# Sliding-window attention on one core: four heads per pipeline stage instead of two, and some small VectorE work placed elsewhere

## The chip, the cores and the metric

One core of a Trainium2 chip runs one program. The metric is the device time of one execution in microseconds, the median of several runs.

## What is computed

Three layers in a row, on 2 sequences of 768 tokens, 8 heads of 64, all in float32. The inputs are drawn at random; the window is 128 tokens and the first 4 tokens are sinks that every query sees.

```python
scores = scale * np.matmul(q, k.transpose(0, 1, 3, 2))
keep = is_sink | in_window
scores = np.where(keep, scores, -1000000000.0)
a = np.exp(scores - np.max(scores, axis=-1, keepdims=True))
a = a / (np.sum(a, axis=-1, keepdims=True) + 1e-09)
x = np.matmul(a, v)                      # 1536 tokens x 512
logits = x @ w_gate                      # 8 experts
# each token goes to the expert of its best pair that still has room (192 each),
# pairs taken by falling logit over all tokens
out[mask] = np.maximum(x[mask] @ w1[e], 0.0) @ w2[e]
x = out
return (x @ w_a) * (x @ w_b) @ w_out     # 512 -> 1536 -> 512
```

## The kernel before

The program has three parts, one behind the other. The attention (`Attention.run`, line 261) leaves the rows of `x` in a DRAM buffer `xd` and the gate's logits in a tile `L`. The routing (`Clear`) finds, in a fixed number of passes over `L`, which token goes where. The experts (`Experts.run`) gather the rows and do all the large products. Every order is written out by hand: each engine works through its instructions in the order in which the code issues them, and waits where an operand or a buffer isn't there yet.

The attention goes over 12 blocks of 128 queries, 6 for each sequence. A block sees its own 128 keys, the 128 before and, from the third block on, 32 keys of the start that hold the sinks: 288 columns. The first block of a sequence sees 128 columns and the second 256, without a sink slice. Queries and keys are each split into a rounded part and the remainder, so a score product is two matmuls into one PSUM tile (lines 281 and 282). `split` (line 248) does that for a block: VectorE casts, GpSimd subtracts (lines 256 to 259). For the first two blocks `split_half` (line 234) does it for four heads at a time: ScalarE casts for block 0 and VectorE for block 1, and GpSimd takes three of the four subtractions of line 245.

A stage `s` of the loop is two heads, so a block is four stages, and a group of four heads is two. In a stage the loop issues, in this order:
- every fourth stage, the loads of a later block on the SP queue (`load_v`, `load`), and the `split` of a later block;
- in odd stages `out_rows` of the group before the last: VectorE multiplies the finished rows by the reciprocal of the softmax sum (line 351), sums the logits (line 354), and the SP queue stores the rows into `xd` (line 355). For the first group of a block VectorE first adds 1e-9 to the sums (line 348) and takes the reciprocal (line 349);
- `scores` three stages ahead: for each of the two heads the two matmuls into a tile `sp` (three PSUM buffers, one for each head), VectorE's masked minimum `mn` (line 283), ScalarE's exponential with its sum (line 285);
- `turn` one stage ahead: four transposes of the probabilities on TensorE (line 297), one ScalarE copy (line 299);
- in odd stages `turn_sink`: the sink columns of four heads turned by matmuls 32 wide (line 307), a VectorE copy (line 309);
- `values` of two stages ago: products of 64 columns for each head (line 324), and with sinks one product 128 wide for the pair (line 327). In odd stages the finished tile `ot` goes to SBUF, on ScalarE for the first group of a block and on VectorE for the second (line 331);
- in even stages `rows`: two products that turn the group's output back to rows and add the gate logits (line 340), into the tile `x` (one buffer).

What else runs in certain stages hangs in a table handed to `run` (line 98): constants of the routing on GpSimd (stage 12), `rest`, four small VectorE operations (stage 30, lines 432 to 435), `lead(0)` to `lead(3)` (stages 36 to 42), and the first sums of the routing (44, 45). `lead` (line 760) loads two pieces of an expert's weights on the SP queue, casts one on ScalarE (line 752) and subtracts on GpSimd (line 758).

Of the kernel before, what the change touches and what calls it, by code (L numbers as in the profile page):

```python
# [22 lines left out]
E, FF = 8, 1024  # L23
# [38 lines left out]
def moe_attention_kernel(ctx: ExitStack, tc: tile.TileContext, kq, vN, vS, nums, wg, w12, wm, out,  # L62
# [22 lines left out]
    with ExitStack() as st:  # L85
        at.open(st, pre)
        at.load(0)

        warm = const.tile([128, 1], F32, name="warm")
        nc.vector.memset(warm, 0.0)  # L90
        nc.scalar.activation(warm, warm, AF.Exp)
        nc.scalar.dma_start(num, dram_ap(nums.bitcast(U32), 0, [[0, 128], [1, 4]]))
        make_identity(nc, ident)
        nc.vector.tensor_copy(numf[:, 0:4:2], num[:, 0:4:2])
        nc.vector.tensor_copy(numf[:, 1:4:2], num[:, 1:4:2].bitcast(I32))
        nc.vector.scalar_tensor_tensor(nv, numf[:, 1:4:2], 4294967296.0, numf[:, 0:4:2], op0=OP.mult, op1=OP.add)
        at.masks(nv[:, 0:1], nv[:, 1:2], slow)
        at.run({12: lambda: cl.constants(at.at), 30: lambda: cl.rest(), 36: lambda: ew.lead(0), 38: lambda: ew.lead(1), 40: lambda: ew.lead(2), 42: lambda: ew.lead(3), 44: lambda: cl.start(at), 45: lambda: cl.rest0(at.pp.tile([128, 128], F32, name="ts", bufs=1)[:, :E])})
# [43 lines left out]
class Attention:  # L142
# [118 lines left out]
    def run(self, extra):  # L261
        nc, at, pp, ident = self.nc, self.at, self.pp, self.ident
        blocks, V, VS, Q, KH, KL = self.blocks, self.V, self.VS, self.Q, self.KH, self.KL
        P, PK, MN, SM, T, TP, ST, OT, OS, XR, LP, RS, X = ({} for _ in range(13))

        nb = len(blocks)
        n = 4 * nb

        def scores(s):
            i, hp = divmod(s, 4)  # L270
            b, j = blocks[i]
            c0, w, co, cp, cs = kwin(j)
            if hp == 0:
                MN[i] = at.tile([128, H], F32, name="mn", bufs=3)
                SM[i] = at.tile([128, H], F32, name="sm", bufs=4)
            if hp % 2 == 0:
                P[s // 2] = at.tile([128, 4, 288], F32, name="p", bufs=3)
            p = P[s // 2]
            for h in (2 * hp, 2 * hp + 1):
# [5 lines left out]
                nc.scalar.activation(p[:, h % 4, :w], p[:, h % 4, :w], AF.Exp, bias=MN[i][:, h:h + 1], scale=-1.0,  # L285
                                     accum_out=SM[i][:, h:h + 1])

        def turn(s):
            i, hp = divmod(s, 4)
            c0, w, co, cp, cs = kwin(blocks[i][1])  # L290
            p = P[s // 2]
            tp = pp.tile([128, 4, 128], F32, name="tp", bufs=2)
            nsl = 2 if cp is None else 4
            for t in range(nsl):
                hl = 2 * (hp % 2) + t % 2
                c = co if t < 2 else cp
                nc.tensor.transpose(tp[:, t], p[:, hl, c:c + 128], ident)
            T[s] = at.tile([128, 4, 128], F32, name="t", bufs=5)
            nc.scalar.activation(T[s][:, :nsl], tp[:, :nsl], AF.Copy)
            if hp % 2 == 1 and cs is not None:  # L300
                PK[s // 2] = p[:, :, cs:cs + NS]

        def turn_sink(g):
            if g in PK:
                sp = pp.tile([128, 128], F32, name="ts", bufs=1)
                for h in range(4):
                    nc.tensor.matmul(sp[NS * h:NS * h + NS], PK[g][:, h], ident, start=True, stop=True, skip_group_check=True)
                ST[g] = at.tile([128, 128], F32, name="st", bufs=3)
                nc.vector.tensor_copy(ST[g], sp)

        def values(s):
            i, hp = divmod(s, 4)
            b, j = blocks[i]
            c0, w, co, cp, cs = kwin(j)
            if hp % 2 == 0:
                OT[s // 2] = (pp.tile([128, 288], F32, name="sp", bufs=3)[:, :256].rearrange("p (a n) -> p a n", a=2) if s == n - 2
                              else pp.tile([128, 2, 128], F32, name="ot", bufs=1))
            o = OT[s // 2]
            first = hp % 2 == 0
            mm = [(V[i], 0)] + ([(V[i - 1], 2)] if cp is not None else [])  # L320
            for k, (v, t) in enumerate(mm):
                for a in range(2):
                    h = 2 * hp + a
                    nc.tensor.matmul(o[64 * a:64 * a + 64, hp % 2], v[:, h * D:(h + 1) * D], T[s][:, t + a],
                                     start=first and k == 0, stop=cs is None and k == len(mm) - 1, skip_group_check=True)
            if cs is not None:
                nc.tensor.matmul(o[:, hp % 2], VS[b][:, hp // 2, hp % 2], ST[s // 2],
                                 start=False, stop=True, skip_group_check=True)
            if hp % 2:
                os = OS[s // 2] = at.tile([128, 2, 128], F32, name="os", bufs=2)  # L330
                (nc.vector.tensor_copy if hp == 3 else nc.scalar.copy)(os, OT.pop(s // 2))

        def rows(g):

            i, q = divmod(g, 2)
            x = X[g] = (pp.tile([128, 288], F32, name="sp", bufs=3).rearrange("p (a n) -> p a n", a=2) if g == n // 2 - 1
# [5 lines left out]
        def out_rows(g):  # L342
            i, q = divmod(g, 2)
            x = X.pop(g)
            if q == 0:
# [4 lines left out]
            hs = slice(4 * q, 4 * q + 4)  # L350
# [9 lines left out]
        for s in range(-3, n + 6):  # L360
            if (s + 3) % 4 == 0:
                i = (s + 3) // 4
# [4 lines left out]
            if (s + 3) % 4 == 1 and (s + 3) // 4 + 2 < nb and s > 0:  # L367
                self.split((s + 3) // 4 + 2, nc.gpsimd)
            if s - 5 >= 0 and s % 2 and (s - 5) // 2 != n // 2 - 2 and (s - 5) // 2 < n // 2:
                out_rows((s - 5) // 2)  # L370
            if s == n + 2:
                out_rows(n // 2 - 2)
            if s == -3:
                self.split_half(0, 0, nc.scalar.copy, nc.vector)()
                rest = self.split_half(0, 1, nc.scalar.copy, nc.gpsimd)
            if 0 <= s + 3 < n:
                scores(s + 3)
            if s == -3:
                rest()
            elif s == -2:  # L380
                self.split_half(1, 0, nc.vector.tensor_copy, nc.gpsimd)()
                self.second()
            elif s == -1:
                self.split_half(1, 1, nc.vector.tensor_copy, nc.gpsimd)()
            elif s == 0:
                self.split(2, nc.gpsimd)
                self.others()
            elif s == 40:
                self.wide()
            if 0 <= s + 1 < n:  # L390
                turn(s + 1)
            if s % 2 == 1 and 0 <= s < n:
                turn_sink(s // 2)
            if 0 <= s - 2 < n:
                values(s - 2)
            if s - 4 >= 0 and s % 2 == 0 and s != n and (s - 4) // 2 < n // 2:
                rows((s - 4) // 2)
            if s == n + 1:
                rows(n // 2 - 2)
            if s in extra:  # L400
                extra[s]()
# [690 lines left out]
```

## Time and profile before

| | us |
|---|---|
| median of 3 runs | 652.66 |
| lowest and highest | 652.20, 653.37 |
| the profiled execution | 653.24 |
| its span, first to last instruction | 651.5 |

| stretch of the profiled execution | from | to |
|---|---|---|
| start, until the scores of block 2 | 8.55 | 33.51 |
| attention, steady | 33.51 | 127.09 |
| tail, from the last group's scores to the last logits | 127.09 | 141.56 |
| routing | 141.56 | 179.49 |
| experts | 179.49 | 651.50 |

In the rows below PE is TensorE's matmuls and PEld its weight loads, DVE is VectorE, ACT is ScalarE, POOL is GpSimd, SP is the queue that issues loads and stores. Times are microseconds from the start of the span. TensorE's order is best read from the weight loads: each belongs to one matmul, and their starts aren't modelled.

### The profile page before, as it was taken

To read this page: it belongs to the slowest core of one execution; us is meant where nothing else is said; L and a number is where in the kernel's file an instruction comes from. 1 tells how busy PE (TensorE), PEld (TensorE's weight loads), DVE (VectorE), ACT (ScalarE), POOL (GpSimd) and SP (SyncE) were. 2 spreads that over 40 slices of the span, in tenths; PEclk is the share of its full clock that TensorE was granted. 3 is DMA by queue.
4 is the path that set the end of the run, shared out by engine and by line. 5 is a ranking of instruction groups with operands and counts; after the bars stand their busy time and mean duration, and the time that the engine had idled before them with its cause. 6 is when DMAs were issued, how large, how long until landed. Compare 5 with 4: busy or idle time off the path is not lost.

```text
span 651.5 us, 10366 instructions
## 1 busy us (share of the span) xinstructions
PE 589.8 (91%) x3804; PEld 544.4 (84%) x3804; DVE 373.0 (57%) x926; ACT 246.3 (38%) x639; POOL 105.2 (16%) x150
## 2 busy tenths in 40 slices
PE   2699969962299999999999999999999999999996
PEld 2478857851299999999999999999999999998885
DVE  6787795658534666756653355655665555722230
ACT  3566656820035445454432223223233223322330
POOL 3757663302311001000000000000000000003021
PEclk9999997985589999999999999999999999999998
DMA  9988673640076777777730023222232222102010
GB/s 187 226 162 198 139 168 99 193 122 9 24 207 212 239 253 235 259 227 246 235 101 2 33 64 98 65 73 89 66 98 64 65 69 93 33 1 97 1 65 33
DMA packets 50284, 79.04 MB, mean 121 GB/s; under 512 B 17456, under 2 KB 25648, under 8 KB 49712
## 3 DMA queue, kind: packets, MB, share of 16 engines
q1 hardware_dynamic: 48160, 71.99, 39.5%
q0 software_dynamic: 1920, 6.29, 3.1%
q8 instruction: 32, 0.52, 0.3%
q14 instruction: 28, 0.23, 0.1%
q10 hardware_dynamic: 144, 0.00, 0.0%
HBM read 71.98 MB, written 6.29 MB: 120 GB/s over the span
## 4 chain that ended last, share of the span: by engine, by line
PE 62%; issue 7%; POOL 1%; DVE 0%; ACT 0%; POOLq 0%
PE b L842 13%; PE b L897 10%; PE b L895 10%; PE b L896 10%; PE b L856 7%; PE b L857 3%; PE b L919 3%; PE b L918 3%; PE b L917 2%; POOL out L935 1%; PE b L832 1%; PE b L947 1%; DVE ys L866 0%; ACT y L868 0%; POOLq L1088 0%
## 5 line engine op out<-in xcount | busy, mean ns | idle before, releaser
L897 PE MATMUL b<-y,ml 128*128 128x384 f32 x384 | 128.6, 335 | 0.0
L895 PE MATMUL b<-y,mh 128*128 128x384 f32 x384 | 128.6, 335 | 0.0
L896 PE MATMUL b<-y,mh 128*128 128x384 f32 x384 | 128.5, 335 | 0.0
L842 PE MATMUL b<-xm,wr 128*128 128x192 f32 x512 | 89.1, 327 | 0.1
L842 PEld LDWEIGHTS b<-xm,wr 128*128 128x128 f32 x512 | 82.4, 190 | 0.3 <-issue 0.3
L856 PE MATMUL b<-hh,wh 128*128 128x384 f32 x256 | 79.5, 374 | 0.0
L895 PEld LDWEIGHTS b<-y,mh 128*128 128x128 f32 x384 | 72.1, 188 | 1.1
L896 PEld LDWEIGHTS b<-y,mh 128*128 128x128 f32 x384 | 72.1, 188 | 1.0
L897 PEld LDWEIGHTS b<-y,ml 128*128 128x128 f32 x384 | 72.1, 188 | 0.0
L758 DVE TENSOR_TENSOR wl<-wr,wh 128x512 fp32r<-128x512 f32 x60 | 41.5, 691 | 41.7 <-ACT wh L752 40.1
L935 POOL DMA_INDIRECT out<-xg,idx x6 | 6.2, 1041 | 361.9 <-ACT xg L933 361.0
L857 PE MATMUL b<-hh,wl 128*128 128x192 f32 x256 | 64.1, 250 | 0.0
L285 ACT ACTIVATE p<-p,mn 128x288 f32<-128x288 f32 (+2 forms) x96 | 47.9, 500 | 41.1 <-DVE mn L283 40.8
L281 PE MATMUL sp<-KH,q 128*128 128x288 f32 (+2 forms) x96 | 34.2, 369 | 22.7 <-DVE mn L283 13.1
L857 PEld LDWEIGHTS b<-hh,wl 128*128 128x128 f32 x256 | 48.9, 191 | 0.0
L856 PEld LDWEIGHTS b<-hh,wh 128*128 128x128 f32 x256 | 48.1, 188 | 0.0
L281 PEld LDWEIGHTS sp<-KH,q 128*128 128x128 f32 x96 | 20.4, 213 | 26.3 <-DVE mn L283 15.0
L283 DVE CUSTOM_DVE_ANT_0 p<-sp,mk 128x288 f32<-128x288 f32 (+2 forms) x96 | 36.8, 419 | 9.6 <-PE sp L282 9.3
L752 ACT ACTIVATE wh<-wr 128x512 fp32r<-128x512 f32 x64 | 39.9, 623 | 3.3 <-DMA wr<-in_w 3.3
L844 ACT ACTIVATE hh<-b 128x192 fp32r<-128x192 f32 x64 | 21.0, 328 | 46.8 <-PE b L842 46.8
L906 ACT ACTIVATE zz<-z 128x384 fp32r<-128x384 f32 x24 | 12.6, 525 | 58.8 <-DVE z L901 58.8
L257 POOL TENSOR_TENSOR KL<-kq,KH 128x1024 fp32r<-128x1024 f32 (+1 forms) x10 | 29.0, 2898 | 35.0 <-DVE KH L256 34.9
(246 smaller groups left out, 1067.8 us busy)
## 6 DMA issues: line engine op xcount, KB each, us to landing
wr<-in_w SPq DMA_DIRECT2D x128, 256.0 KB, 3.9
mr<-in_wm SPq DMA_DIRECT2D x36, 512.0 KB, 3.6
kq<-in_kq SPq DMA_DIRECT2D x12, 512.0 KB, 7.6
kq<-in_kq SPq DMA_DIRECT2D x8, 576.0 KB, 9.8
v<-in_vN SPq DMA_DIRECT2D x12, 256.0 KB, 4.9
xd<-xr SPq DMA_DIRECT2D x12, 256.0 KB, 3.2
kq<-in_kq SPq DMA_DIRECT2D x8, 256.0 KB, 6.2
xg<-xd,idx POOLq DMA_INDIRECT x12, 4.0
```

Of the source, the lines that this page charges most:

```text
L257: eng.tensor_tensor(kl, kr, kh.bitcast(F32), op=OP.subtract)
L281: nc.tensor.matmul(sp[:, :w], Q[i][:, h], KH[:, h, c0:c0 + w], start=True, stop=False)
L283: nc.vector.tensor_tensor_reduce(p[:, h % 4, :w], sp[:, :w], self.mask(j), -0.125, 1e30, op0=OP.add, op1=OP.min, accum_out=MN[i][:, h:h + 1])
L285: nc.scalar.activation(p[:, h % 4, :w], p[:, h % 4, :w], AF.Exp, bias=MN[i][:, h:h + 1], scale=-1.0, accum_out=SM[i][:, h:h + 1])
L752: self.nc.scalar.activation(self.W[u][0], self.R[u, 1], AF.Copy)
L758: (eng or self.nc.vector).tensor_tensor(lo, self.R.pop((u, 1)), hi.bitcast(F32), op=OP.subtract)
L842: nc.tensor.matmul(ps, w[:, 128 * k:128 * k + 128], x[:, k], start=k == 0, stop=k == 3)
L856: nc.tensor.matmul(ps, hi[:, 128 * d:128 * d + 128], hh, start=f == 0, stop=False, skip_group_check=True)
L857: nc.tensor.matmul(ps[:, 0], lo[:, 128 * d:128 * d + 128], hh[:, 0], start=False, stop=f == 7, skip_group_check=True)
L895: nc.tensor.matmul(p, hi[:, w, c], y[:, k, 0], start=k == 0, stop=False)
L896: nc.tensor.matmul(p, hi[:, w, c], y[:, k, 1], start=False, stop=False)
L897: nc.tensor.matmul(p, lo[:, w, c], y[:, k, 0], start=False, stop=k == 3)
```

## The change

Nothing of the arithmetic changes. A stage is now a group of four heads; iteration `it` issues `out_rows` of group `it - 3`, the scores of group `it + 1`, the turns of `it`, the values of `it - 1` and the rows of `it - 2`. ScalarE's instructions of a stage are held in lists and issued in a chosen order: two exponentials, the first copy of the turned probabilities, two exponentials, the second copy. The buffers keep their numbers. The add of 1e-9 goes from VectorE to ScalarE. In the first two blocks all subtractions are on VectorE and all casts on ScalarE. A `split` is issued behind the scores in even iterations. The table of other work goes to the iterations of the same groups: `rest` to 15, `lead` to 18 to 21.

```diff
-        at.run({12: lambda: cl.constants(at.at), 30: lambda: cl.rest(), 36: lambda: ew.lead(0), ...})
+        at.run({6: lambda: cl.constants(at.at), 15: lambda: cl.rest(), 18: lambda: ew.lead(0), 19: lambda: ew.lead(1), ...})
...
+        def scores(g):
+            i, q = divmod(g, 2)
...
+            out = []
+            for h in range(4 * q, 4 * q + 4):
                 sp = pp.tile([128, 288], F32, name="sp", bufs=3)
                 nc.tensor.matmul(sp[:, :w], Q[i][:, h], KH[:, h, c0:c0 + w], start=True, stop=False)
                 nc.tensor.matmul(sp[:, :w], Q[i][:, h], KL[:, h, c0:c0 + w], start=False, stop=True)
                 nc.vector.tensor_tensor_reduce(p[:, h % 4, :w], sp[:, :w], self.mask(j), -0.125, 1e30, op0=OP.add,
                                                op1=OP.min, accum_out=MN[i][:, h:h + 1])
+                out.append(lambda h=h: nc.scalar.activation(...))
+            return out
...
+            for e in range(2):
+                for k, (v, t) in enumerate(mm):
+                    for a in range(2):
+                        h = 4 * q + 2 * e + a
+                        nc.tensor.matmul(o[64 * a:64 * a + 64, e], v[:, h * D:(h + 1) * D], T[g, e][:, t + a], ...)
             if cs is not None:
+                for e in range(2):
+                    nc.tensor.matmul(o[:, e], VS[b][:, q, e], ST[g], start=False, stop=True, skip_group_check=True)
+            os = OS[g] = at.tile([128, 2, 128], F32, name="os", bufs=2)
+            return lambda: (nc.vector.tensor_copy if q else nc.scalar.copy)(os, o)
...
-                nc.vector.tensor_scalar(r[:, 0], SM[i], 1e-9, None, op0=OP.add)
+                nc.scalar.activation(r[:, 0], SM[i], AF.Identity, bias=tiny)
                 nc.vector.reciprocal(r[:, 1], r[:, 0])
...
+        self.split_half(0, 0, nc.scalar.copy, nc.vector)()
+        for it in range(-1, ng + 2):
+            if it % 2 and (it + 1) // 2 < nb:
+                i = (it + 1) // 2
                 if i + 1 < nb:
                     self.load_v(i + 1)
                 if i + 3 < nb:
                     self.load(i + 3)
+            if 0 <= it - 3:
+                out_rows(it - 3)
+            exps = scores(it + 1) if it + 1 < ng else []
+            for e in exps[:2]:
+                e()
+            if it == -1:
+                self.split_half(0, 1, nc.scalar.copy, nc.vector)()
+            elif it == 0:
                 self.second()
+                for half in range(2):
+                    self.split_half(1, half, nc.scalar.copy, nc.vector)()
+            elif it == 1:
+                self.others()
                 self.split(2, nc.gpsimd)
+            elif it % 2 == 0 and it // 2 + 2 < nb:
+                self.split(it // 2 + 2, nc.gpsimd)
+            ts = turn(it) if 0 <= it < ng else []
+            for e in ts[:1]:
+                e()
+            for e in exps[2:]:
+                e()
+            for e in ts[1:]:
+                e()
+            if 0 <= it < ng:
+                turn_sink(it)
+            if 0 <= it - 1 < ng:
+                copy = values(it - 1)
+            if 0 <= it - 2 < ng:
+                rows(it - 2)
+            if 0 <= it - 1 < ng:
+                copy()
+            if it == 20:
                 self.wide()
+            if it in extra:
+                extra[it]()
+        out_rows(ng - 1)
```

## Rows read from the trace of the kernel before

**Rows 1.** Table of stretches: length, busy time of each engine, granted clock, transfers.

```profile
core 0: us, PE busy (x) PEld busy (x) DVE busy (x) ACT busy (x) POOL busy (x), PEclk, DMA share, GB/s
8.55:33.51 24.96, 15.36 (x64) 12.12 (x64) 18.32 (x50) 12.15 (x47) 14.81 (x7) 1.00 1.08 226
33.51:70.47 36.96, 36.45 (x356) 29.77 (x356) 29.27 (x102) 26.49 (x84) 26.24 (x58) 1.00 0.78 168
70.47:107.92 37.45, 31.45 (x267) 24.78 (x266) 29.46 (x91) 20.16 (x70) 17.56 (x7) 0.91 0.61 133
107.92:127.09 19.17, 19.17 (x194) 15.67 (x193) 11.92 (x55) 15.01 (x46) 7.73 (x5) 1.00 0.65 192
127.09:141.56 14.47, 13.65 (x139) 10.34 (x137) 7.30 (x29) 6.62 (x20) 1.75 (x2) 1.00 0.36 94
...
179.49:651.50 472.01, 465.43 (x2664) 445.21 (x2664) 246.93 (x468) 161.35 (x364) 22.24 (x33) 0.99 0.37 115
```

**Rows 2.** Timeline of weight loads, one group: start, length, instruction, idle before and releaser.

```profile
48.82 0.19 PEld L281 LDWEIGHTS sp<-KH,q 128*128 128x128 f32 x1
...
49.33 0.48 PEld L297 LDWEIGHTS tp<-ident,p 128*128 128x128 f32 x4
49.98 0.42 PEld L324 LDWEIGHTS ot<-t,v 128*64 128x64 f32 x8 [0.17 <-ACT os L331]
50.56 0.30 PEld L327 LDWEIGHTS ot<-st,vs 128*128 128x128 f32 x2 [0.17 <-DVE rs L348]
50.78 0.55 PEld L340 LDWEIGHTS x<-ig,os 128*128 128x128 f32 x4
51.26 0.19 PEld L281 LDWEIGHTS sp<-KH,q 128*128 128x128 f32 x1
...
52.44 0.16 PEld L307 LDWEIGHTS ts<-ident,p 128*32 128x32 f32 x8 [0.17 <-issue]
52.80 0.42 PEld L324 LDWEIGHTS ot<-t,v 128*64 128x64 f32 x8 [0.20 <-issue]
...
53.60 0.19 PEld L281 LDWEIGHTS sp<-KH,q 128*128 128x128 f32 x1
```

**Rows 3.** Timeline of VectorE at three places, last a weight load that waits.

```profile
51.59 0.46 DVE L351 TENSOR_TENSOR xr<-x,rs 128x288 f32<-128x288 f32 x1 [0.84 <-PE x L340]
51.96 0.45 DVE L283 CUSTOM_DVE_ANT_0 p<-sp,mk 128x288 f32<-128x288 f32 x1
...
117.81 0.46 DVE L351 TENSOR_TENSOR xr<-x,rs 128x288 f32<-128x288 f32 x1 [1.30 <-PE x L340]
...
118.49 0.45 DVE L283 CUSTOM_DVE_ANT_0 p<-sp,mk 128x288 f32<-128x288 f32 x1
...
97.39 0.45 DVE L283 CUSTOM_DVE_ANT_0 p<-sp,mk 128x288 f32<-128x288 f32 x1
...
97.90 0.19 PEld L281 LDWEIGHTS sp<-KH,q 128*128 128x128 f32 x1 [4.00 <-DVE mn L283]
```

**Rows 4.** Groups by line and shape up to 33.51 us: busy, mean ns, idle before.

```profile
L259 POOL TENSOR_TENSOR q<-kq,q 64x1024 fp32r<-64x1024 f32 x2 | 4.8, 2406 | 0.2
L257 POOL TENSOR_TENSOR KL<-kq,KH 128x1280 fp32r<-128x1280 f32 x1 | 3.3, 3258 | 2.5 <-DVE KH L256 2.5
L191 DVE TENSOR_SCALAR mk<-mk 128x576 f32<-128x576 f32 x1 | 3.1, 3137 | 0.0
L245 DVE TENSOR_TENSOR KL<-kq,KH 128x512 fp32r<-128x512 f32 x1 | 0.7, 692 | 1.3 <-ACT KH L243 1.3
```

**Rows 5.** The add of line 348 (ns, min/median/max), and the first of `rest`.

```profile
L348 DVE TENSOR_SCALAR rs<-sm x12: 160/426/2043, 31.6 to 139.9; 128x8 f32<-128x8 f32 x12
...
92.18 2.26 DVE L432 SCALAR_TENSOR_TENSOR dg<-er,ak 128x128 f32<-128x128 f32 x1
```

**Rows 6.** Timeline of the weight loads of `lead` on SP and their casts on ScalarE.

```profile
114.13 0.63 ACT L752 ACTIVATE wh<-wr 128x512 fp32r<-128x512 f32 x1 [1.19 <-DMA wr<-in_w]
...
118.88 8.08 SPq L746 DMA_DIRECT2D wr<-in_w  x8
...
124.62 0.63 ACT L752 ACTIVATE wh<-wr 128x512 fp32r<-128x512 f32 x1 [2.08 <-DMA wr<-in_w]
```

More of the change, by code (lines that the diff above doesn't have):

```diff
@@ L97, in moe_attention_kernel @@
         at.masks(nv[:, 0:1], nv[:, 1:2], slow)
-        at.run({12: lambda: cl.constants(at.at), 30: lambda: cl.rest(), 36: lambda: ew.lead(0), 38: lambda: ew.lead(1), 40: lambda: ew.lead(2), 42: lambda: ew.lead(3), 44: lambda: cl.start(at), 45: lambda: cl.rest0(at.pp.tile([128, 128], F32, name="ts", bufs=1)[:, :E])})
+        at.run({6: lambda: cl.constants(at.at), 15: lambda: cl.rest(), 18: lambda: ew.lead(0), 19: lambda: ew.lead(1), 20: lambda: ew.lead(2), 21: lambda: ew.lead(3), 22: lambda: cl.start(at), 23: lambda: cl.rest0(at.pp.tile([128, 128], F32, name="ts", bufs=1)[:, :E])})
     redo = pre.tile([128, 1], I32, name="redo")
@@ L284, in scores @@
                                                op1=OP.min, accum_out=MN[i][:, h:h + 1])
[L285 to L289, printed above, removed]
+                out.append(lambda h=h: nc.scalar.activation(p[:, h % 4, :w], p[:, h % 4, :w], AF.Exp, bias=MN[i][:, h:h + 1],
+                                                            scale=-1.0, accum_out=SM[i][:, h:h + 1]))
@@ L290, in turn @@
+            return out
+        def turn(g):
+            i, q = divmod(g, 2)
             c0, w, co, cp, cs = kwin(blocks[i][1])
-            p = P[s // 2]
-            tp = pp.tile([128, 4, 128], F32, name="tp", bufs=2)
+            p = P[g]
             nsl = 2 if cp is None else 4
[L294 to L298, printed above, removed]
@@ L299, in turn @@
-            nc.scalar.activation(T[s][:, :nsl], tp[:, :nsl], AF.Copy)
-            if hp % 2 == 1 and cs is not None:
-                PK[s // 2] = p[:, :, cs:cs + NS]
+            out = []
+            for e in range(2):
+                tp = pp.tile([128, 4, 128], F32, name="tp", bufs=2)
+                for t in range(nsl):
+                    c = co if t < 2 else cp
+                    nc.tensor.transpose(tp[:, t], p[:, 2 * e + t % 2, c:c + 128], ident)
+                t = T[g, e] = at.tile([128, 4, 128], F32, name="t", bufs=5)
+                out.append(lambda t=t, tp=tp: nc.scalar.activation(t[:, :nsl], tp[:, :nsl], AF.Copy))
@@ L303, in turn_sink @@
+            return out
         def turn_sink(g):
-            if g in PK:
+            i, q = divmod(g, 2)
+            cs = kwin(blocks[i][1])[4]
+            if cs is not None:
                 sp = pp.tile([128, 128], F32, name="ts", bufs=1)
                 for h in range(4):
-                    nc.tensor.matmul(sp[NS * h:NS * h + NS], PK[g][:, h], ident, start=True, stop=True, skip_group_check=True)
+                    nc.tensor.matmul(sp[NS * h:NS * h + NS], P[g][:, h, cs:cs + NS], ident, start=True, stop=True, skip_group_check=True)
@@ L308, in turn_sink, with values @@
                 ST[g] = at.tile([128, 128], F32, name="st", bufs=3)
                 nc.vector.tensor_copy(ST[g], sp)
-        def values(s):
-            i, hp = divmod(s, 4)
+        def values(g):
+            i, q = divmod(g, 2)
             b, j = blocks[i]
             c0, w, co, cp, cs = kwin(j)
[L315 to L319, printed above, removed]
-            mm = [(V[i], 0)] + ([(V[i - 1], 2)] if cp is not None else [])
[L321 to L325, printed above, removed]
-            if cs is not None:
[L327 to L331, printed above, removed]
@@ L366, in run @@
                     self.load(i + 3)
[L367 to L381, printed above, removed]
+            if 0 <= it - 3:
[6 more added lines that the diff above has]
+            elif it == 0:
```

44 lines of the change are left out of this document (13 added, 31 removed).

## The prediction

> **What bounds the kernel now.** I read the table of stretches first [rows 1]. Behind 179.49 us TensorE is busy for 465.43 of 472.01 us at clock 0.99, and nothing that the change touches runs there. The routing between 141.56 and 179.49 us is not touched either. So only the attention, up to 141.56 us, can move the end, and what it loses or gains moves everything behind it by as much. In it the stretches differ: from 107.92 to 127.09 TensorE is busy without a break (19.17 of 19.17), from 33.51 to 70.47 nearly so (36.45 of 36.96), but the start uses 15.36 of 24.96 us and the stretch from 70.47 to 107.92 uses 31.45 of 37.45 at a mean clock of 0.91. So TensorE's own sequence is the bound in the steady part, and waits are in the start and in the middle.
>
> The second view is the weight loads of TensorE over one group of four heads [rows 2]: 48.82 to 53.60, 4.78 us. The brackets matter: TensorE stands 0.17 us at the first value product (128x64 tiles), 0.17 at the sink product (128x128), 0.17 at the sink turn (128x32) and 0.20 at the value product behind it, whichever releaser the row names; where the tile width stays (scores behind rows, turns behind scores) it stands not at all. The value products are issued twice in a group, so there are five such gaps (the fifth is like the second).
>
> The third view is VectorE beside it [rows 3]. A row product `x` is out 0.33 us after the next scores begin (51.26, 51.59), and the first score reduction follows 0.37 later (51.96). Where the logit sum stands between, it is 0.68 later (117.81, 118.49). From the start of a reduction until TensorE may write its score buffer again it takes 0.51 us (97.39, 97.90).
>
> **What the change does, part by part.**
>
> *Fewer switches.* With four heads per stage, the values of both pairs stand together. Of the five gaps in a group two go: turn to values, and values to sink or rows. 2 x 0.17 = 0.34, so TensorE's sequence for a group falls from 4.78 to 4.44 us. A group without sinks has four gaps and keeps two, the same 0.34.
>
> *A new wait.* `sp` still has three buffers, but a stage now has four heads. The fourth head's scores must wait until VectorE has reduced the first head's, and VectorE first does `out_rows` of three stages ago, whose `x` TensorE wrote just before. Two heads take 0.51 us (48.82 to 49.33) [rows 2], so TensorE is at the fourth head 0.77 us after the stage began. It may go on at 0.33 + 0.37 + 0.51 = 1.21 us in odd iterations and at 0.33 + 0.68 + 0.51 = 1.52 us in even ones [rows 2, 3]. That is 0.43 and 0.74 us of standing. Queued behind on TensorE are this stage's turns, the sink turn, the values and the rows: the whole sequence. An odd iteration becomes 4.87 us, an even one 5.18: in the mean 5.03 against 4.78. The switches saved are more than paid back. Bounds: nothing, if VectorE were there sooner, up to 1.0 if its products came late as well; I take the rows' own sum because the program's order leaves VectorE no choice.
>
> *Work out of GpSimd's way.* The add of 1e-9 takes 0.16 us undisturbed and up to 2.04 us [rows 5]; on ScalarE it should cost 0.2 us and hide there, but the reciprocal, and all that VectorE has queued behind it, now waits for ScalarE's queue. The four operations of `rest` stay on VectorE, at the end of iteration 15. In the kernel before, the first took 2.26 us beside a GpSimd subtraction [rows 5], and TensorE then stood 4.00 us, up to 97.90 [rows 3], with the lower clock after it. (The Trainium skill, "SBUF — State Buffer", section on the two separate sides, says that VectorE and GpSimd share one port pair, which the first comer holds for its whole instruction, against VectorE operations with two SBUF inputs or in a two-port mode. The rows agree, 2.26 us for 128 elements; by that rule `dg`, with two SBUF inputs, is held again wherever a split runs.) Block 9's subtractions begin about 3.2 us into iteration 14 and last about 5.1 (an estimate, a little under the 3.26 + 2.41 of a wider block) [rows 4], so until about 4.4 us into iteration 15, of 3.9 us and 4.1 us length. `rest` reaches VectorE at 2.3 us in iteration 15, waits to 4.4, and ends at 5.3, 1.2 into iteration 16. The fourth head's wait there becomes 1.6 us instead of 0.74. So most of the stall goes, not all.
>
> *ScalarE's wait for weights.* `lead(0)` and `lead(2)` copy a weight that is asked for only behind the `xd` store of the same iteration. The weight came 5.74 us after the issue (118.88 to 124.62) [rows 6]. Now the store's product is ready at about 0.8 us, the weight is asked for at 1.4 and lands at 7.2, which is 2.0 us into the next, odd iteration. There ScalarE still has to copy (0.55) and add (0.2), then VectorE takes the reciprocal (0.2) and the product (0.37): the first reduction starts at 3.3 instead of 0.70, 2.6 us late, all of it TensorE's. In the kernel before, ScalarE waited too (1.19 and 2.08 us) [rows 6] and TensorE did not, since no VectorE work of the row stage hung on ScalarE. For the first weight, whose wait was 0.9 us shorter, I take 1.7. Bounds: nothing, and 2.6 each.
>
> *The start.* It is a chain, from 8.55 us, which stays. Two exponentials and two casts on ScalarE to about 11.2, then two subtractions on VectorE at 0.69 [rows 4]: the second half of block 0 is ready at 12.6 (about 1 us later than now). Four score blocks and reductions to 15.0, masks 0.9, four subtractions at 0.69 and a little between them: block 1 is ready at 18.7. Two more exponentials, six mask copies on ScalarE to 21.3, the wide mask operation, which took 3.14 us beside GpSimd [rows 4], now about 0.4 before it, the cast of block 2 to 22.6, then GpSimd 3.26 + 2.41 [rows 4]: block 2 is ready at 28.4. TensorE's own work before it (stages 0 to 3) ends at the same time by its slower rows. So block 2's scores begin at 28.5 instead of 33.51: -5.0 us. Bounds: -6.5, if the copies overlap better; 0, if a load or the low speed of the first products holds block 2. GpSimd gets no subtraction of blocks 0 and 1; what hides VectorE's four is nothing, they are on the path and counted.
>
> **The sum**, by the stretches of rows 1, against the profiled 653.24 us (span 651.5):
> - start: -5.0.
> - 33.51 to 70.47, eight groups, 36.96 us: the first 3.65 and 0.9 for slower products (the start's take 15.36 us for 64 records, the next stretch's 36.45 for 356, though the clock column reads 1.00 in both), the second, with no sink product yet, 4.0 + 0.74, then three odd at 4.87 and three even at 5.18: 39.4. +2.5.
> - 70.47 to 107.92, seven groups, 37.45 us. With scores at 0.13 us each, turns at 0.12, values 0.42 for eight, sink product 0.22 for a pair, row product 0.48 [rows 2], and blocks 6 and 7 narrower and without sinks: TensorE's sequences 4.36, 3.53, 2.70, 3.17, 3.64, 4.01, 4.44 = 25.9, and waits at the fourth head 0.32, 0.62, 0.44, 0.74, 0.49, 1.63, 0.43 = 4.7: 30.5. -6.9, most of it the 4.00 us stall and the slow stretch after it.
> - 107.92 to 127.09, four groups, 19.17 us: 5.18 + 4.87 + 5.18 + 4.87 and 1.7 + 2.6 for the weights: 24.4. +5.2.
> - the tail, 14.47 us: 5.18 for the last scores, 3.4 for a stage without them, 1.6 for the last values, 2.4 from them to the last logits: 12.6. -1.9.
>
> Together -6.1: the profiled execution would take 647.1. The median of the runs shown, 652.66, is 0.6 below that execution, so I predict 646.5.
>
> **Rivals.**
> - *The fourth head does not wait.* Then all its waits go, 4.3 + 4.7 + 2.3 + 0.7 = 12 us: 634.5. For it: VectorE is busy for only 11.92 of 19.17 us where TensorE is the bound [rows 1]. Against it: the order on VectorE is fixed, and the product in front of the reduction needs a TensorE result that is 0.33 us old at best. Chance 0.08.
> - *The stalls bring the clock down (slower than before).* The middle stretch ran at 0.91, which is 0.09 x 37.45 = 3.4 us lost behind one stall of 4.00 us. Now TensorE stands for 1.6, 2.1 and 3.0 us in iterations 16, 19 and 21. If a stall of 1.6 is enough, three times 3.4 gives +10: 656.7; if only the two longer ones are, 653.3. Against it: the stalls are shorter than the one that did it, and no row here shows where it begins. Chance 0.11.
> - *The start does not pay.* Block 2 begins when it did, because the loads or TensorE's slow first products set it (the transfer engines are busy the whole time, share 1.08): 651.5. Chance 0.10.
> - *The add is moved but VectorE gains nothing by it.* If ScalarE reaches the add half a microsecond late in each of the twelve odd iterations, VectorE waits there and TensorE behind it: +6, 652.5. Against it: ScalarE is busy for 15.01 of 19.17 us even where it copies weights [rows 1]. Chance 0.06.
>
> **How the numbers follow.** The forecast, 646.5, has 0.65, with a range of its own of 641 to 651: the start by 2, the wait per group by 0.1 us over 23 groups, the weights by 3. For 8 in 10 I leave out the first rival (0.08), the upper half of the second and the forecast's own tails: 640 to 654. A measurement of this kernel tells about 0.2% from no change, 1.3 us. Faster than 651.4: 0.63 from the forecast, 0.08 from the first rival, 0.08 from the lower sides of the others: 0.79. Slower than 654.0: 0.08 from the second rival and 0.03 from the last two: 0.11. The rest, 0.10, lies between.
>
> **What would show it.** In the profile of the changed kernel: three gaps of 0.17 to 0.20 us at TensorE in a group instead of five; a wait of the fourth head's first score product for VectorE's `mn`, 0.4 to 0.8 us, in nearly every group, and group periods that alternate around 4.9 and 5.2 us; block 2's scores at about 28.5 us; a short VectorE hold at `dg`; a wait of the reciprocal for ScalarE behind the first and third weight; the last logits at about 135.4 us. If the periods are near 4.5, the first rival holds; if weight loads show the lower clock behind iteration 16, 19 or 21, the second; if block 2 begins near 33, the third. The prediction is wrong if the periods lie above 5.3 or if the clock falls.

## The result and the profile after

The change made the kernel slower: 656.52 us (median of 5 runs, 655.07 to 656.67) against 652.66 (5 runs, 651.37 to 653.73), a ratio of 1.0053 with a 95% interval of 1.0035 to 1.0072. Forecast was 646.5, with a range of 640 to 654. The profiled execution of the changed kernel has a span of 654.8 us, against 651.5 before.

The table of stretches of the changed kernel, cut where the same groups of four heads begin as in [rows 1], with the columns of that table.

```profile
8.62:34.52 25.90, 12.47 (x67) 10.49 (x68) 15.64 (x49) 14.16 (x52) 10.64 (x4) 0.87 1.08 224
34.52:74.85 40.33, 37.75 (x369) 32.02 (x369) 25.86 (x98) 27.57 (x88) 22.03 (x56) 0.96 0.70 150
74.85:105.74 30.89, 27.34 (x267) 22.98 (x265) 22.36 (x87) 21.70 (x77) 20.14 (x9) 1.00 0.75 161
105.74:131.74 26.00, 20.41 (x195) 16.98 (x194) 12.74 (x53) 15.67 (x48) 8.88 (x5) 0.93 0.54 163
131.74:144.44 12.70, 11.42 (x121) 9.48 (x119) 6.79 (x26) 5.77 (x17) 1.74 (x2) 1.00 0.27 64
```

Beside the forecast this gives, in us:

| stretch | before | forecast | after | after less forecast |
|---|---|---|---|---|
| start, to the scores of block 2 | 24.96 | 19.95 | 25.90 | +6.0 |
| blocks 2 to 5 | 36.96 | 39.4 | 40.33 | +0.9 |
| blocks 6 to 8 and half of 9 | 37.45 | 30.5 | 30.89 | +0.4 |
| the next four groups | 19.17 | 24.4 | 26.00 | +1.6 |
| tail | 14.47 | 12.6 | 12.70 | +0.1 |

Four of the five rows came out within 1.6 us of the forecast. The start did not: it was to give 5.0 us and took 0.9. The timeline of weight loads of the changed kernel shows where (start, length, instruction, idle before and releaser):

```profile
33.64 0.98 PEld L341 LDWEIGHTS x<-ig,os 128*128 128x128 f32 x4 [8.53 <-issue]
34.52 0.34 PEld L282 LDWEIGHTS sp<-KH,q 128*128 128x128 f32 x1
...
39.73 0.19 PEld L282 LDWEIGHTS sp<-KH,q 128*128 128x128 f32 x1
```

TensorE stands for 8.53 us ahead of its first row product (line 341), with the scores of block 2 queued behind it. The name in the bracket is `issue`, so the row alone doesn't tell what was late. The view of the product's weight tile `ig` does (who idled until what; the time from issue to landing of its loads):

```profile
  DMA ig<-in_wg: 8.3, 1
...
DMA to landing us min/median/max: 11.0/11.2/11.3
```

`ig` holds the gate's weights, which two loads of 8 KB each bring. The SP queue of the changed kernel in that time (start, time to issue, line, how many):

```profile
19.78 0.55 SPq L228 DMA_DIRECT2D v<-in_vN  x1
20.66 1.12 SPq L220 DMA_DIRECT2D kq<-in_kq  x2
21.83 1.29 SPq L193 DMA_DIRECT2D ig<-in_wg  x2
```

and of the kernel before:

```profile
19.70 1.66 SPq L193 DMA_DIRECT2D ig<-in_wg  x2
21.40 0.60 SPq L228 DMA_DIRECT2D v<-in_vN  x1
22.11 1.13 SPq L220 DMA_DIRECT2D kq<-in_kq  x2
```

The two gate loads are issued by `others` (line 193). Before, `others` ran ahead of the loads of values and keys; now it runs in iteration 1 behind them. The two loads left 2.1 us later, and they landed 11.2 us after the issue, behind block 4's keys, instead of 6.2. (The Trainium skill, "DMA: Bandwidth & Descriptors", section on queues, rings and completion order, says that each engine takes the descriptors of a ring in order; the two traces agree, 11.2 us behind the keys and 6.2 ahead of them.)

In the steady part the changed kernel does what the forecast said [rows 2, 3]. One group of four heads, weight loads:

```profile
54.58 0.19 PEld L282 LDWEIGHTS sp<-KH,q 128*128 128x128 f32 x1
...
55.91 0.19 PEld L282 LDWEIGHTS sp<-KH,q 128*128 128x128 f32 x1 [0.50 <-DVE mn L284]
...
57.25 0.16 PEld L311 LDWEIGHTS ts<-ident,p 128*32 128x32 f32 x8 [0.17 <-issue]
57.61 0.85 PEld L326 LDWEIGHTS ot<-t,v 128*64 128x64 f32 x16 [0.20 <-issue]
58.63 0.52 PEld L330 LDWEIGHTS ot<-st,vs 128*128 128x128 f32 x4 [0.17 <-issue]
...
59.55 0.19 PEld L282 LDWEIGHTS sp<-KH,q 128*128 128x128 f32 x1
...
61.06 0.19 PEld L282 LDWEIGHTS sp<-KH,q 128*128 128x128 f32 x1 [0.67 <-DVE mn L284]
```

Three gaps of 0.17 to 0.20 us are left of five, and the fourth head waits 0.50 or 0.67 us for VectorE's reduction (forecast 0.43 and 0.74). The periods are 4.97 and 5.15 (forecast 4.87 and 5.18), against 4.78 before.

### The profile page after: what moved, and what is told of

Read it like the earlier page. It is cut to its first block, busy times and chain, and to the rows that moved or that the text cites. A ratio compares the mean times of both kernels' runs of the same rounds, so it can differ in the third digit from the quotient of the medians.

```text
span 654.8 us, 10355 instructions
## 1 busy us (share of the span) xinstructions
PE 583.6 (89%) x3804; PEld 544.2 (83%) x3804; DVE 359.9 (55%) x913; ACT 250.9 (38%) x655; POOL 100.4 (15%) x148
## 4 chain that ended last, share of the span: by engine, by line
PE 62%; issue 7%; POOL 1%; DVE 0%; ACT 0%; POOLq 0%
PE b L845 13%; PE b L900 10%; PE b L898 10%; PE b L899 10%; PE b L859 7%; PE b L860 3%; PE b L922 3%; PE b L921 2%; PE b L920 2%; POOL out L938 1%; PE b L835 1%; PE b L950 1%; DVE ys L869 0%; ACT y L871 0%; POOLq L1091 0%
## 5 line engine op out<-in xcount | busy, mean ns | idle before, releaser
L909 ACT ACTIVATE zz<-z 128x384 fp32r<-128x384 f32 x24 | 12.6, 525 | 58.8 <-DVE z L904 58.8
```

## The experiments

All are edits of the changed kernel, except where an edit of the kernel before is named. "Group" is four heads; its time is read from the first score product of one to the first of the next.

### The start: where the gate loads stand on the SP queue

**e1_gate_load_first.** The two gate loads leave `others` for a function of their own, called in iteration 0, ahead of block 4's keys.

```diff
+        def gate():
...
             elif it == 0:
                 self.second()
+                self.gate()
...
```

> Only the place of the two small gate-weight loads on the SP queue is changed: issued in iteration 0, ahead of block 4's keys, as in the kernel before. Theory (the start lost its gain because the first row product waited for these loads behind 1.2 MB of keys): they land near 26 us, TensorE stands 1 to 2 us instead of 8.5, block 2's scores begin at 28 to 29 us instead of 34.5, and the clock does not fall there; 6 to 7 us less than the changed kernel's 656.5, so 649.5 to 650.5. Rival (the start is held by block 2's keys, GpSimd's subtractions or slow products anyway): block 2 begins at 32 or later and the time is 654 or more.

Measured: 652.12 us (650.22 to 653.35), a ratio to before of 0.9997 (0.9983 to 1.001). Block 2's scores begin at 28.27 us, but the row product ahead of them still stands for 1.99 us, and the products behind run at the slow pace: the group takes 7.22 us instead of 4.55. So the loads' place is the cause of the 8.53 us, but mending it gave 4.4 us by the medians, where 6 to 7 were expected.

**e9_gate_at_once.** The same loads ahead of the first value load, before the loop starts, so that no row product can wait for them.

```diff
         self.load(2)
+        self.gate()
         self.load_v(0)
```

> The changed kernel with the two gate loads issued on the SP queue ahead of the first value load, before the loop. In the earlier run with them in iteration 0 the row products still stood 1.99, 0.60 and 1.07 us in the start. Theory (the queue position of these two loads is the whole failed step of the start): no row product waits for the gate; block 2's scores at 28.2 us, the group behind them at 34.4 (39.73 in the changed kernel), so 5.3 us less: 650.5 to 651.5, since the two stalls of 2.98 and 2.19 us at the weights stay. Rival (the half-speed products of the start set it, whenever the gate comes): the group behind starts at 35.5 as in the earlier run and the time stays at 652.

Measured: 651.76 us (650.78 to 654.18), 0.999 (0.9978 to 1.0002), no better than the first try. (Its profiled execution took 654.18 us, 2.4 more than the median.) Its weight loads:

```profile
28.32 0.19 PEld L284 LDWEIGHTS sp<-KH,q 128*128 128x128 f32 x1 [2.41 <-POOL q L261]
...
31.12 0.29 PEld L284 LDWEIGHTS sp<-KH,q 128*128 128x128 f32 x1 [1.51 <-DVE mn L286]
...
33.60 1.58 PEld L328 LDWEIGHTS ot<-t,v 128*64 128x64 f32 x16 [0.33 <-issue]
...
35.95 0.19 PEld L284 LDWEIGHTS sp<-KH,q 128*128 128x128 f32 x1
```

VectorE's timeline beside it:

```profile
28.39 0.69 DVE L258 CAST KH<-kq 128x1024 fp32r<-128x1024 f32 x1 [3.94 <-DMA kq<-in_kq]
```

The gate loads land 11.3 us after the issue, behind six loads of keys, but well before they are needed. The row product's stall is gone, and block 2's scores begin at 28.32 us, released by GpSimd's last subtraction: the 28.5 of the forecast. But the next group begins at 35.95, not at 33.05 as the forecast's sum has it (28.5 and a first group of 3.65 + 0.9). Two things take the 7.63 us of that group. Sixteen weight loads of value products take 1.58 us instead of 0.85; the table of stretches of this run agrees (granted clock in the third column from the end):

```profile
26.00:28.30 2.30, 0.13 (x2) 0.00 (x0) 0.00 (x0) 0.75 (x3) 2.27 (x1) 1.00 1.24 255
28.30:31.00 2.70, 1.63 (x6) 1.28 (x6) 2.51 (x8) 0.00 (x0) 1.78 (x1) 0.55 0.97 197
```

0.55 is near the lower of the two levels, 1.2 of 2.4 GHz; ahead of it TensorE stood 2.41 us. And the fourth head waits 1.51 us, since VectorE stood 3.94 us for block 3's keys, whose loads the queue now issues at 20.03 us instead of 16.54. Of the two theories for this run the second held in its numbers: with the gate on time, the slow products set the time, and beside them VectorE's wait, which it had not named.

### The score buffer

**e2_rows_behind.** VectorE's work on the rows is issued behind this iteration's score reductions instead of ahead of them; the buffers stay three.

```diff
-            if 0 <= it - 3:
-                out_rows(it - 3)
             exps = scores(it + 1) if it + 1 < ng else []
             for e in exps[:2]:
                 e()
+            if 0 <= it - 3:
+                out_rows(it - 3)
```

> Only the row stage's VectorE and ScalarE work (add, reciprocal, product, logit sum) is issued behind the score reductions instead of ahead of them. Theory (the fourth head waits for VectorE because the row product stands in front of the first reduction): the wait falls from 0.50 and 0.67 us to about 0.3 in every group, and the two long stalls behind the expert weights (2.98 and 2.19 us) go, since the reciprocal no longer stands in front of the reductions: 8 to 9 us less, 647.5 to 648.5. Rival (the order on VectorE is not what sets the wait): 655 or more, waits of 0.5 us and over stay.

Measured: 648.6 us (648.47 to 649.35), 0.9942 (0.9921 to 0.9963), 8 us below the changed kernel. The wait is 0.26 or 0.27 us in most groups (in three it is 1.01, 1.43 and 0.65), as here:

```profile
58.10 0.19 PEld L282 LDWEIGHTS sp<-KH,q 128*128 128x128 f32 x1
...
59.20 0.19 PEld L282 LDWEIGHTS sp<-KH,q 128*128 128x128 f32 x1 [0.26 <-DVE mn L284]
...
62.84 0.19 PEld L282 LDWEIGHTS sp<-KH,q 128*128 128x128 f32 x1
```

The period is 4.74 in place of 4.97 and 5.15, and the two stalls at the expert weights are gone; in their place row products wait 1.22 and 1.54 us. So VectorE's order makes the larger part of the wait; the 0.26 us that stay are those of three buffers, and go with a fourth (the next run).

**e3_sp4.** A fourth score buffer; for its room in PSUM the tiles `ts` and `x` share a bank.

```diff
+        self.tx = self.pp.tile([128, 512], F32, name="tx")
...
-                sp = pp.tile([128, 288], F32, name="sp", bufs=3)
+                sp = pp.tile([128, 288], F32, name="sp", bufs=4)
...
-                sp = pp.tile([128, 128], F32, name="ts", bufs=1)
+                sp = self.tx[:, 288:416]
...
```

> A fourth score buffer: the sink turn and the row product share one PSUM bank, and the bank that comes free becomes a fourth buffer; the order stays. Theory (the three buffers are the cause of the wait at the fourth head): all waits of TensorE for a reduction go, also those of 2.98, 2.19, 1.22 and 1.02 us, the group period falls to about 4.45 us, 13 to 16 us less: 640.5 to 643.5, with the 8.5 us at the first row product still in it. Rival (VectorE's and ScalarE's own work per stage is the bound as soon as the wait goes): the period stays at 4.9 to 5.1, no more than 4 us less, 652 or more.

Measured: 647.88 us (647.09 to 649.65), 0.9937 (0.9915 to 0.996), 4 us above what was expected. The periods are the expected ones, 4.45 and 4.53, with no wait at the fourth head. But the shared bank makes new waits wherever VectorE is late:

```profile
98.00 0.54 PEld L342 LDWEIGHTS tx<-ig,os 128*128 128x128 f32 x4 [2.14 <-DVE st L314]
...
111.10 0.16 PEld L312 LDWEIGHTS tx<-ident,p 128*32 128x32 f32 x8 [1.67 <-DVE xr L353]
```

The first stands behind `rest`, whose first operation took 2.40 us there; the second behind the first expert weight. A fourth buffer takes away the wait that is there in every group and leaves those whose cause is elsewhere.

### The stalls at the expert weights

In the changed kernel, ScalarE at the two of them, iterations 19 and 21:

```profile
112.69 0.63 ACT L755 ACTIVATE wh<-wr 128x512 fp32r<-128x512 f32 x1 [2.31 <-DMA wr<-in_w]
...
124.53 0.63 ACT L755 ACTIVATE wh<-wr 128x512 fp32r<-128x512 f32 x1 [1.52 <-DMA wr<-in_w]
125.06 0.28 ACT L350 ACTIVATE rs<-sm,tiny 128x8 f32<-128x8 f32 x1
```

VectorE at the second:

```profile
125.38 0.20 DVE L351 RECIPROCAL rs<-rs 128x8 f32<-128x8 f32 x1 [0.79 <-ACT rs L350]
```

The weight loads that wait, at the first and at the second:

```profile
114.72 0.19 PEld L282 LDWEIGHTS sp<-KH,q 128*128 128x128 f32 x1 [2.98 <-DVE mn L284]
...
126.56 0.27 PEld L282 LDWEIGHTS sp<-KH,q 128*128 128x128 f32 x1 [2.19 <-DVE mn L284]
```

It is the chain that the prediction gave: the weight is late, ScalarE waits to copy it, the add stands behind the copy, the reciprocal behind the add, the reduction behind that, TensorE behind the reduction.

**e4_weights_sooner.** The loads of the first three weights two iterations sooner.

```diff
+16: lambda: [ew.load_w(u, a) for u in range(3) for a in range(2)],
...
-        for a in range(2):
-            self.load_w(u, a)
         self.hi_w(u)
         self.lo_w(u, self.nc.gpsimd)
+        if u == 0:
+            for a in range(2):
+                self.load_w(3, a)
```

> Only the loads of the first three expert weights are issued two iterations sooner. Theory (ScalarE, waiting for a weight, holds the add, the reciprocal behind it, and so TensorE): the stalls of 2.98 and 2.19 us become 0.5, and the slow stretch behind the second goes: 5 to 6 us less, 650.5 to 651.5. Rival (these stalls come from GpSimd's weight subtraction holding VectorE): the stalls stay, 655.5 or more.

Measured: 651.69 us (650.48 to 654.57), 0.9994 (0.9979 to 1.001). The stall of 2.98 us became 0.56, but the other only went from 2.19 to 2.06, though ScalarE now copied in time. VectorE there:

```profile
120.33 0.90 DVE L201 TENSOR_TENSOR c<-nv 128x1 f32<-128x1 f32 x1
...
121.58 0.19 DVE L351 RECIPROCAL rs<-rs 128x8 f32<-128x8 f32 x1
```

Ahead of the reciprocal stands `wide`, five operations on a single column (lines 199 to 203) that iteration 20 issues last. One of them, 0.15 us in the changed kernel, took 0.90 beside GpSimd's subtraction of the weight.

**e10_three_mended.** The gate loads at once, the weights sooner, and `wide` ahead of the copy of `os`, where VectorE waits for TensorE anyhow. The order of the rest is the changed kernel's.

```diff
...
+            if it == 20:
+                self.wide()
             if 0 <= it - 1 < ng:
                 copy()
-            if it == 20:
-                self.wide()
```

> The changed kernel with three things mended and its order of work otherwise kept: the gate loads ahead of the first value load, the first three expert weights loaded two iterations sooner, and the five small VectorE operations of `wide` issued in iteration 20 ahead of the copy of os instead of behind it. With the weights sooner alone, the second stall (iteration 21) stayed at 2.06 us of 2.19; there the reciprocal followed the end of `wide` at 121.58, one of whose operations took 0.90 us beside GpSimd. Theory (that stall had two causes, the weight and `wide`): now the second stall is 0.5 to 0.7 us, and the time is 651 - 4 - 1.5: 645.0 to 646.5, about what the prediction gave. Rival (the add on ScalarE alone holds the reciprocal): the second stall stays at about 2 us and the time is 647.

Measured: 645.46 us (644.58 to 646.7), 0.9887 (0.9869 to 0.9905). The second stall is 0.57 us, as the first:

```profile
108.22 0.19 PEld L284 LDWEIGHTS sp<-KH,q 128*128 128x128 f32 x1 [0.57 <-DVE mn L286]
...
118.43 0.19 PEld L284 LDWEIGHTS sp<-KH,q 128*128 128x128 f32 x1 [0.57 <-DVE mn L286]
```

So that stall had two causes, one behind the other; the second showed only when the first was gone. The four groups that took 26.00 us take 20.41 here.

### The add, and `rest`

**e7_add_on_vector.** The add of 1e-9 back on VectorE.

```diff
-                nc.scalar.activation(r[:, 0], SM[i], AF.Identity, bias=tiny)
+                nc.vector.tensor_scalar(r[:, 0], SM[i], 1e-9, None, op0=OP.add)
```

> The changed kernel with the add of 1e-9 back on VectorE, nothing else. Theory (VectorE would be held there until GpSimd's key subtraction ends, 1.0 to 1.6 us into an odd iteration): the add takes 0.8 to 1.4 us in most odd iterations, the fourth head's wait there grows by as much, about 9 times, against 5 to 6 us saved behind the two expert weights: 3 to 7 us more than the changed kernel's 656.5. Rival (VectorE isn't held): the add takes 0.16 us and the time falls by 5 to 6, to 650.5 to 651.5.

Measured: 665.46 us (663.96 to 668.35), 1.0192 (1.0164 to 1.022), 9 us above the changed kernel, where 3 to 7 were expected. The add in the view of the tile `rs` (min/median/max ns):

```profile
L350 DVE TENSOR_SCALAR rs<-sm x12: 159/737/2044, 29.9 to 154.5; 128x8 f32<-128x8 f32 x12
```

The timeline of VectorE at one of the long adds:

```profile
100.72 2.00 DVE L350 TENSOR_SCALAR rs<-sm 128x8 f32<-128x8 f32 x1
...
103.42 0.45 DVE L284 CUSTOM_DVE_ANT_0 p<-sp,mk 128x288 f32<-128x288 f32 x1
```

Where GpSimd runs, the add takes up to 2.04 us, and the reductions stand behind it. Here TensorE's fourth head waits 2.44 us, the granted clock of the group is 0.78, and the group takes 7.71 us; odd groups whose add is held for only 0.73 us take 5.75 instead of 4.97. In the changed kernel ScalarE's twelve adds lie between 0.285 and 0.303 us. (The Trainium skill, "SBUF — State Buffer", section on who interferes with whom, says that operations like this one and like a cast can enter a mode that needs the port pair shared with GpSimd, and that the one that comes second is then blocked until the other's instruction is done. The rows agree: GpSimd's subtraction runs from 100.00 to 102.70 us, and the add, 0.16 us undisturbed [rows 5], from 100.72 to 102.72.) So in the new order the move of the add is worth 9 us; no run makes it in the order before.

**e6_before_rest_33.** The kernel before, with `rest` three stages later and nothing else.

```diff
-12: lambda: cl.constants(at.at), 30: lambda: cl.rest(),
+12: lambda: cl.constants(at.at), 33: lambda: cl.rest(),
```

> The kernel before, with one thing changed: the four small VectorE operations for the routing's constants in stage 33 instead of 30, when GpSimd has no subtraction running. Theory (the middle stretch lost about 7 us to these operations being held beside GpSimd and to the slow clock after it; the grouping has no part in that gain): 6 to 7 us less than before's 652.2, 645.5 to 646.5. Rival (the grouping itself made that gain, or another operation stalls there next): 651 or more.

Measured: 646.25 us (645.79 to 646.9), 0.9905 (0.9882 to 0.9928). In its table of stretches, the one that answers to 70.47 to 107.92 [rows 1]:

```profile
70.49:100.91 30.42, 28.45 (x267) 22.74 (x266) 26.41 (x87) 19.74 (x69) 16.67 (x7) 1.00 0.74 163
```

30.42 us, where the changed kernel has 30.89 and the kernel before 37.45. Its first operation of `rest` took 0.28 us, beside no GpSimd subtraction. So moving `rest` alone gives as much in the middle as the whole change; four heads in a stage aren't needed for it.

### Versions that beat both

**e5_all** (four score buffers, early gate and weight loads, `rest` in iteration 17), **e8_orders** (three buffers, rows behind the reductions, the same early loads and `rest`) and **e11_wide_ahead** (the same as e8_orders, with `wide` ahead of the copy). Their edits are those shown above, and:

```diff
-15: lambda: cl.rest(),
+17: lambda: cl.rest(),
```

> The changed kernel with four score buffers, the gate loads ahead of the values of block 0, the expert weights' loads two iterations sooner, and the four operations of the routing's constants in iteration 17, whose group has a sink turn so that VectorE comes to them later. Theory (the losses are these separate waits and add up): against the kernel with four buffers alone (647.9) the start gives 3 to 6, the two expert-weight stalls 3, the stretch at iterations 15 to 17 about 3: 636 to 640. Rival (one wait covers the next): 644 or more.

> The changed kernel with its three score buffers, but the row stage's VectorE work behind the reductions, the gate loads ahead of the values of block 0, the expert weights' loads two iterations sooner, the routing's constants in iteration 17. Theory: a wait of 0.26 us in every group stays, the other stalls go: against 648.6 of the kernel with the row stage behind, the start gives 3 to 6 and the expert weights and the constants 3 more: 639.5 to 643. Rival (one wait covers the next): 646 or more.

> The version with rows behind the reductions, early gate and weight loads and `rest` in iteration 17 (640.75), with `wide` issued in iteration 20 ahead of the copy of os. Its last long stall is 1.40 us at 113.33, where VectorE was in `wide` from 111.26 to 112.83. Theory (that stall is `wide`): it becomes about 0.3 and the time is 639.0 to 640.0. Rival (the stall is something else): no difference, 640.7.

Measured: 639.54 us (638.99 to 640.54), a ratio to before of 0.98 (0.9778 to 0.9822); 640.75 (639.18 to 642.3), 0.9818 (0.9787 to 0.9848); 640.54 (638.81 to 641.21), 0.9808 (0.9791 to 0.9825). The three can't be told apart. The first two lie within what was expected of them: the separate losses add up. In e11_wide_ahead the stall of 1.40 us in iteration 21 is gone and its group takes 4.74 us instead of 5.88, but the start came out 0.7 us longer in its profiled execution, and the time didn't show the gain; so that theory is shown for the stall and not for the time.

## Why the prediction was wrong

The span came out 9.4 us above the forecast for the profiled execution (647.1, its span 645.4): 6.0 in the start, 0.9, 0.4, 1.6 and 0.1 in the other stretches, 0.4 behind the attention.

**The step that failed is the start.** The prediction followed the chain over ScalarE, VectorE and GpSimd, and that chain came true: the second half of block 0 is ready at 12.61 us (forecast 12.6), and with the gate mended block 2's scores begin at 28.32 (28.5). What it left out are the DMAs inside `others`: its sentence "block 2 is ready at 28.4" speaks of the scores' operands, and "TensorE's own work before it (stages 0 to 3) ends at the same time" took for granted that the row products had theirs. Counted to the start of the group behind, 39.73 us against a forecast of 33.05, the miss is 6.7: 39.73 to 35.95, 3.8 us, is the gate loads' place (e9_gate_at_once), and 35.95 to 33.05, 2.9, is what stays when they are on time. Two things make that rest. VectorE's wait for block 3's keys, 1.51 us, was not in the sum. And the products were sized too small: the group's 7.63 us less that wait are 6.12, where the sum had 3.65 and 0.9 for their slowness, so the 0.9 measured 2.5. e5_all, whose four buffers leave no wait at the fourth head, shows the products alone, 6.41 us for the same group:

```profile
28.21 0.29 PEld L285 LDWEIGHTS sp<-KH,q 128*128 128x128 f32 x1 [3.77 <-POOL q L262]
...
34.62 0.19 PEld L285 LDWEIGHTS sp<-KH,q 128*128 128x128 f32 x1
```

In the changed kernel that group took 5.21 us, most of the 0.9 in the table's second row. Nor did TensorE's earlier work end when block 2 was ready: in e9_gate_at_once TensorE had stood for 2.41 us by then. (These parts are of single executions: by the medians, 656.52 and 651.76, the loads' place is worth 4.8 us, not 3.8.)

The bound at the worse end, "0, if a load or the low speed of the first products holds block 2", was the right one. The third rival was built on it, and a load did hold block 2, though the rival named none; block 2 began at 34.52 us, where the rival had it as before, at 33.51.

**The switches and the new wait: right.** 2 x 0.17 us less, 0.50 and 0.67 of standing, periods of 4.97 and 5.15. The rival that the fourth head doesn't wait is out; e2_rows_behind and e3_sp4 show that it would have paid.

**`rest`: right in kind, and the whole of the middle.** The hold came: VectorE's first operation of `rest` and its fourth in the timeline of the changed kernel:

```profile
93.85 1.97 DVE L435 SCALAR_TENSOR_TENSOR dg<-er,ak 128x128 f32<-128x128 f32 x1
...
96.31 0.17 DVE L438 CAST eh<-ef 128x8 bf16<-128x8 f32 x1
```

and the fourth in the kernel before:

```profile
94.91 1.90 DVE L435 CAST eh<-ef 128x8 bf16<-128x8 f32 x1
```

TensorE's weight loads that wait in that iteration and the next:

```profile
92.86 0.19 PEld L282 LDWEIGHTS sp<-KH,q 128*128 128x128 f32 x1 [1.22 <-DVE mn L284]
...
97.57 0.19 PEld L282 LDWEIGHTS sp<-KH,q 128*128 128x128 f32 x1 [1.02 <-DVE mn L284]
```

1.02 us of waiting, forecast 1.6, against 4.00 before [rows 3]. Before, `rest` was held twice, 2.26 us at its first operation [rows 5] and 1.90 at its fourth, behind GpSimd's two subtractions; the prediction named the first alone. Now there is one hold. That the stretch came out within 0.4 us is partly luck: the group ahead waited 1.22 us where the sum had 0.49, since VectorE's reciprocal there stood 0.36 us for ScalarE and its cast 0.30 us for keys. What the prediction did not say is that this gain doesn't need the grouping; e6_before_rest_33 has it alone.

**The expert weights: the chain right, their sum by luck, plus a clock.** The two stalls were forecast at 2.1 and 3.0 us and measured at 2.98 and 2.19. Each is off by 0.8 or 0.9 us, and the errors cancel: the prediction took the first weight's wait as the shorter, and ScalarE waited 2.31 us for the first and 1.52 for the second. The 1.6 us above the forecast are the lower clock behind the second one, in the table of stretches of the changed kernel:

```profile
114.70:118.40 3.70, 3.68 (x43) 3.15 (x43) 1.39 (x7) 3.36 (x11) 0.86 (x1) 1.00 0.00 0
...
126.50:131.70 5.20, 5.14 (x41) 4.25 (x42) 1.52 (x8) 3.34 (x11) 0.00 (x0) 0.67 0.56 191
```

A third of 5.20 us is 1.7. So the rival of the clock came true in one place out of three, at half the 3.4 us it was priced at; that "the clock falls" was one of the prediction's own signs of being wrong. Why 2.98 us of standing cost nothing here and 2.19 did stays open. It is not the place in the program, for at the same one in e1_gate_load_first the loads behind the stall are slow:

```profile
110.20 0.29 PEld L284 LDWEIGHTS sp<-KH,q 128*128 128x128 f32 x1 [3.11 <-DVE mn L286]
```

In e9_gate_at_once they are too, behind 2.78 us; of the 3.8 us gained at its start, 2.5 are left at the last row products (140.40 us against 142.88). `wide`, which the prediction passed over, cost nothing in the changed kernel, since the late weight hid it.

**The add: right.** It took 0.28 us where 0.2 was put, and ScalarE had room for it in most groups: the reciprocal waited for it in three, 2.39 and 0.79 us at the two weights and 0.36 in iteration 15. The rival that VectorE gains nothing by the move is refuted by 9 us.

**The tail: right**, 12.70 us against 12.6.

So the parts that were worked out from rows of the steady state held to 0.1 us a group, and with three things mended that are not the change's idea (the two gate loads, the loads of three weights, five small operations) the changed kernel runs at 645.46 us, near the 646.5 forecast. That nearness is partly chance: the mended version lacks the weights' stalls that the forecast counted, 4.3 us, and has the slow first group that it did not.

## What to carry to other kernels

When a function is moved past others, write down every DMA it issues and its new place on its queue, small ones too: two loads of 8 KB behind some large ones held TensorE for 8.53 us. When more work is put into a stage, count each buffer against the stage again, and each engine's order within it; and when an operation moves to another engine, whatever that engine waits for becomes a wait of the first one. A stall that doesn't go when its cause is removed may have a second cause that the first one hid.

## What the runs showed of the hardware

- The granted clock can fall behind a stall of some 2 us, but not behind each, and the stall's length alone doesn't say when. It fell behind 2.41 us (e9_gate_at_once, 0.55), behind 2.19 us (0.67) and behind all four stalls of 2.39 to 2.52 us in e7_add_on_vector (0.78 to 0.80 over their groups); it did not behind 2.98 us (1.00), nor behind 2.06 us (e4_weights_sooner, 1.00). It fell behind none of the waits of 0.41 to 1.22 us in the changed kernel's steady part.
- The clock column alone isn't enough at the start of a program: it reads 1.00 up to 28.30 us in e9_gate_at_once, though a weight load there takes 0.29 us at 19.15 and 0.19 from 21.78 on. The length of a weight load is the better sign.
- An operation on a single column, 0.15 us long, took 0.90 us beside a GpSimd subtraction, and an add of 128x8 numbers 2.04: what the operation waits for has nothing to do with its size.
